# Delta-rule attention followed by mixture of depths on one core: another order of the work, six block inverses on VectorE, rank counts on TensorE

## The chip, the cores and the metric

The kernel runs on one core of a Trainium2 chip. Five engines work on their own queues, each in the order in which its instructions were written: TensorE (PE), VectorE (DVE), ScalarE (ACT), GpSimd (POOL) and SyncE (SP, which here only issues DMAs). An instruction that waits holds up everything behind it on its engine. The metric is the device time of one execution in microseconds (us), and the lower the better.

## The reference, cut to what matters

```
# attention: B=4, H=8, S=768, D=48; k_n = k / (|k| + 1e-6); state starts at zero
for t in range(S):
    y[:, :, t] = q[:, :, t] @ state                       # with the state before step t
    v_old = state^T k_n[t]
    state = state + beta[t] * outer(k_n[t], v[t] - v_old)
# bridge: x[b, s] = the 8 heads of y side by side (384 numbers)
# mixture of depths: per batch row b
scores = x[b] @ w_gate                                    # 768 scores
top = the 128 tokens with the largest scores
out[b] = x[b]; out[b, top] += sigmoid(scores[top]) * (relu(x[b, top] @ w1) @ w2)   # 384 -> 1024 -> 384
```

The 768 steps depend on each other, so they are worked in chunks of 64 tokens: inside a chunk the steps are joined through the inverse of a unit triangular 64x64 matrix per head, and only the 48x48 states pass from chunk to chunk.

## The kernel before, in words

**Units.** The batch rows are worked in two groups (rows 0 and 1, then rows 2 and 3), each of 12 chunks: 24 units, 0 to 23. A unit covers one chunk of 64 tokens for 2 rows x 8 heads. `prep` loads k and q, transposes them on TensorE (L388, copied by ScalarE at L392) and forms the products k k^T and k q^T (L405, copied at L414); GpSimd masks the second (L422). `recur` is the chain from state to state: r (L634), the subtraction on DVE (`sub`, L638), w (L646), its copies (L652), s (L660) and the new state (L666). Beside it stand q (L673) and p (L683), whose sum is the output x (L689), written to DRAM (L696). `vh` (L626, DVE) scales V before that.

**Inverses.** The triangular matrices of four units are inverted together, six times: inverse 0 for units 0 to 3, and so on to inverse 5 for units 20 to 23. `eliminate` moves the lower right halves into its buffer `a` by a DVE transpose (`turn_in`, L484; the data are shifted into place by DMA first, L433), takes norms with a root on ScalarE (L490), scales (L509), does 30 elimination steps of two instructions each (L523 and L527), applies the mask table (`final`, L533), and turns the result out (`turn_out`, L537; `turn_back`, L542). `join` (z at L587, j at L598) makes 64x64 inverses out of the 32x32 halves, and then the four units can run. Inverses 0, 2, 4 and 5 run their steps on DVE with one operand in PSUM (`pa`, filled by ScalarE at L514); inverses 1 and 3 (`POOL_E`) run on GpSimd, in SBUF.

**Depths.** `depths(b)` does the mixture for one row: scores (L701 on GpSimd and L708 on ScalarE), all scores spread over the partitions (L771, L780, L787), the rank of each token by comparing and counting on DVE (`ranks`, L813 and L818, in two stages: the first four blocks of 128 tokens, and the other two), the selection (`choose`, L826), its indices (L833), a gather (L848), the two layers on TensorE (L864, L878) with copies on ScalarE, and a scatter that adds the result to the output (L887).

**Order.** The class `Plan` sets the order in which each engine's instructions are written: every piece of work is an `Op` with an engine, a duration that is written down, what it waits for, the buffers it takes and gives back, and a priority given by a formula at each call (`u` in the functions above). `Plan.order` steps through planned time and picks the most urgent piece that can start; `Plan.fill` puts spare matmuls (L963) into planned gaps of TensorE. The three PSUM banks `inv` are shared by nearly all that TensorE makes outside the chain.

Of the kernel before, what the change touches and what calls it, by code (L numbers as in the profile page):

```python
# [25 lines left out]
class Plan:  # L26
# [56 lines left out]
    def fill(self, start, end, done):  # L83

        slots = self.rings["inv"]
        k = min(range(len(slots)), key=lambda x: slots[x])
        t = max(start, slots[k]) + 0.1
        while t + 0.6 < end:
            op = Op()
            op.eng, op.start, op.end, op.take, op.give, op.seq = "PE", t, t + 0.25, k, [], -1  # L90
            self.fills.append(op)
            t += 0.45

    def order(self):
        free, ready, last, done, self.fills = {}, {}, {}, [], []
# [5 lines left out]
        while len(done) < len(self.ops):  # L101
# [10 lines left out]
            if op.eng == "PE":  # L112
                self.fill(free["PE"], at, done)
# [38 lines left out]
def kernel(  # L152
# [57 lines left out]
    POOL_E = (1, 3)  # L210
# [22 lines left out]
    ring("a", 2, [HC, HC])  # L233
# [5 lines left out]
    ring("sel", 1, [NT, P])  # L239
    ring("xe", 2, [DM])  # L240
# [8 lines left out]
    psta = psum.tile([P, GI, 2 * D], FP32, name="psta")  # L249
# [12 lines left out]
    pe, act, dve, pool, sp = [maker(e) for e in ("PE", "ACT", "DVE", "POOL", "SP")]  # L262

# [19 lines left out]
    warm = sbuf("warm", [256], BF16)  # L283
# [18 lines left out]
    tmp = [sbuf(f"tmp{m}", [HC * HC // 4]) for m in range(2)]  # L302
# [10 lines left out]
    def constants():  # L313
# [6 lines left out]
        nc.vector.memset(psta, 0.0)  # L320
# [4 lines left out]
        for t in rings["tt"]:  # L325
# [8 lines left out]
        for t in count:  # L334
            nc.vector.memset(t, 0.0)
# [39 lines left out]
    def gk(e):  # L375
        return "g2" if e == 2 else "g"
# [58 lines left out]

    def prep(i):
        e = i // BC
        u = 40 * (e - 1) + 2 * (i % BC) - 40 * (e in POOL_E)
# [3 lines left out]
        n["lk"] = kq_on[0](1.3, load(i, "k", kq_on[1]), prio=u - 30, take=[("k", i)], lat=2.2)  # L442
# [550 lines left out]
```

## Time and profile before

| | |
|---|---|
| median of 3 runs | 409.05 us (408.43 to 413.15) |
| profiled execution | 409.91 us, its span 408.1 us |
| TensorE, matmuls | 323.1 us busy (79%) |
| TensorE, weight loads | 270.1 us (66%) |
| VectorE | 218.1 us (53%) |
| ScalarE | 179.0 us (44%) |
| GpSimd | 154.3 us (38%) |
| DMA | 32.19 MB, mean 79 GB/s |

The span runs from the first to the last instruction of the execution. Busy times of different engines overlap. No engine is busy all the time, so the shares alone tell no bound: one has to follow which engine works alone at what time. TensorE's clock is granted at one of two levels, 2.4 GHz (1.00 in the rows) and 1.2 GHz (0.50); a number between is the mean over a stretch.

### The profile page before, as it was taken

What the parts mean: (1) busy time and instruction counts of PE and PEld (TensorE: products, weight loads), DVE (VectorE), ACT (ScalarE), POOL (GpSimd) and SP (SyncE); (2) the same over time, 40 slices, a digit from 0 to 9 for tenths busy, and PEclk for the clock granted to TensorE, in tenths of its full rate; (3) what the DMA queues carried; (4) which work ended last, traced back from release to release, by engine and by line L of the source; (5) the groups of instructions that cost most, each with busy time, mean ns of one, the idle gap of its engine ahead of it and who ended that gap; (6) DMA issues with size and microseconds to landing.
All of it is one profiled execution on the core that took longest, in us unless ns stands there. A gap on an engine that the chain in (4) does not pass through costs nothing. (4 is left out here: it accounts for less than half of the span.)

```text
span 408.1 us, 14040 instructions
## 1 busy us (share of the span) xinstructions
PE 323.1 (79%) x5969; PEld 270.1 (66%) x5969; DVE 218.1 (53%) x573; ACT 179.0 (44%) x477; POOL 154.3 (38%) x239
## 2 busy tenths in 40 slices
PE   4885887689738899988489987799905998793993
PEld 3764675578627898976359876698605995663871
DVE  3004889948789211223877778958894006773000
ACT  2342564357724446566356573454202545110120
POOL 5012557888830156986832134021310014111011
PEclk9999776759975558996965899659965568696898
DMA  9847747333567233656742444133311013002011
GB/s 126 140 81 134 133 87 140 62 68 78 111 122 128 44 69 70 189 119 161 181 93 50 88 99 78 29 58 83 59 39 29 2 27 74 1 2 39 19 22 20
DMA packets 141855, 32.19 MB, mean 79 GB/s; under 512 B 139664, under 2 KB 141216, under 8 KB 141792
## 3 DMA queue, kind: packets, MB, share of 16 engines
q1 hardware_dynamic: 134432, 28.64, 35.3%
q0 software_dynamic: 960, 1.59, 2.2%
q10 hardware_dynamic: 6400, 1.05, 1.9%
q8 instruction: 47, 0.77, 0.7%
q14 instruction: 16, 0.13, 0.1%
HBM read 22.61 MB, written 5.51 MB: 69 GB/s over the span
## 5 line engine op out<-in xcount | busy, mean ns | idle before, releaser
L701 POOL TENSOR_TENSOR xw<-x,wg 128x384 f32<-128x384 f32 x23 | 23.5, 1024 | 101.4 <-ACT x L689 99.9
L422 POOL TENSOR_SCALAR_AFFINE_SELECT p<-p 64x512 f32<-64x512 f32 x44 | 31.9, 726 | 43.6 <-ACT p L414 36.9
L523 DVE TENSOR_TENSOR tmp<-a,pa 128x30 f32<-128x30 f32 (+14 forms) x120 | 39.0, 325 | 8.1 <-ACT pa L514 4.7
L527 DVE TENSOR_TENSOR pa<-pa,tmp 128x30 f32<-128x30 f32 (+14 forms) x120 | 40.6, 338 | 4.1
L392 ACT COPY kq<-inv 128x512 f32<-128x512 f32 x44 | 25.2, 589 | 37.6 <-PE inv L388 36.0
L638 DVE TENSOR_TENSOR r<-v,prec 128x384 f32<-128x384 f32 x22 | 12.1, 552 | 54.3 <-PE prec L634 45.6
L405 PE MATMUL inv<-kq 48*64 48x128 f32 (+1 forms) x832 | 37.6, 311 | 2.7 <-ACT p L414 1.6
L626 DVE TENSOR_TENSOR v<-v,nnT 128x384 f32<-128x384 f32 x24 | 19.3, 809 | 32.1 <-DMA v<-in_v_dram 32.0
L405 PEld LDWEIGHTS inv<-kq 48*64 48x64 f32 x832 | 29.1, 172 | 11.0 <-issue 4.5
L646 PE MATMUL prec<-r,tt 64*64 64x48 f32 x704 | 32.0, 251 | 4.2 <-ACT tt L603 2.0
L388 PE MATMUL inv<-ident,q 128*128 128x128 f32 x96 | 21.5, 371 | 16.4 <-DMA q<-in_q_dram 11.6
L527 POOL TENSOR_TENSOR a<-a,tmp 128x30 f32<-128x30 f32 (+14 forms) x60 | 32.7, 545 | 4.7
L813 DVE TENSOR_SCALAR_CACHE_REDUCE junk<-rep,tok 128x256 bf16<-128x256 f32 (+4 forms) x60 | 31.7, 528 | 3.5 <-ACT rep L787 1.5
L587 PE MATMUL inv<-tt,g 32*32 32x32 f32 x640 | 18.4, 227 | 18.6 <-DVE tok L801 13.0
L646 PEld LDWEIGHTS prec<-r,tt 64*64 64x64 f32 x704 | 29.0, 166 | 6.0 <-DVE r L638 2.4
L652 ACT COPY wbd<-prec 64x384 f32<-64x384 f32 x48 | 22.7, 472 | 20.6 <-PE prec L646 19.2
L523 POOL TENSOR_TENSOR tmp<-a 128x30 f32<-128x30 f32 (+14 forms) x60 | 29.4, 490 | 4.1
L388 PE MATMUL inv<-ident,k 128*128 128x128 f32 x96 | 21.3, 367 | 12.1 <-DMA k<-in_k_dram 9.5
L587 PEld LDWEIGHTS inv<-tt,g 32*32 32x32 f32 x640 | 16.6, 141 | 21.0 <-DVE tok L801 13.1
L388 PEld LDWEIGHTS inv<-ident,q 128*128 128x128 f32 x96 | 15.6, 192 | 20.4 <-DMA q<-in_q_dram 6.0
L864 PE MATMUL inv<-xeT,w_sb 128*128 128x128 f32 x192 | 25.9, 299 | 2.0 <-ACT p L414 1.0
L864 PEld LDWEIGHTS inv<-xeT,w_sb 128*128 128x128 f32 x192 | 24.8, 212 | 3.2 <-ACT xeT L858 1.8
(110 smaller groups left out, 619.6 us busy)
## 6 DMA issues: line engine op xcount, KB each, us to landing
v<-in_v_dram SPq DMA_DIRECT2D x48, 96.0 KB
out_dram<-x SPq DMA_DIRECT2D x96, 48.0 KB
k<-in_k_dram SPq DMA_DIRECT2D x44, 96.0 KB
q<-in_q_dram SPq DMA_DIRECT2D x44, 96.0 KB
ks<-in_k_dram SPq DMA_DIRECT2D x44, 96.0 KB
tt<-tt SPq DMA_DIRECT2D x12, 128.0 KB
w_sb<-in_moe_w_dram SPq DMA_DIRECT2D x4, 384.0 KB
w_sb<-in_moe_w_dram SPq DMA_DIRECT2D x3, 512.0 KB
```

The source lines that it names most:

```text
L388: nc.tensor.transpose(ps[:, r * P:(r + 1) * P], x[:, 2 * r:2 * r + 2].rearrange("p b d -> p (b d)"), ident)
L392: nc.scalar.copy(got(kk(i), i)[:, :, o], got("inv", i, nm).rearrange("p (r t) -> p r t", t=P))
L405: nc.tensor.matmul(bank(i, w, rt)[half[par], r, o], lhsT=kq[ds[rt], r, 0, half[par]], rhs=kq[ds[rt], r, o, half[par]], start=True, stop=True)
L422: nc.gpsimd.affine_select(out=t[half[par]], in_=t[half[par]], pattern=[[0, GP], [1, C]], base=0, channel_multiplier=-1, compare_op=ALU.is_ ...
L523: eng.tensor_tensor(out=t, op=ALU.mult, in0=a[:, j + 1:, j:j + 1].to_broadcast([P, w, j]), in1=x[:, j:j + 1, :j].to_broadcast([P, w, j]))
L527: eng.tensor_tensor(out=x[:, j + 1:, :j], in0=x[:, j + 1:, :j], in1=t, op=ALU.subtract)
L587: nc.tensor.matmul(ps[lo[par], b], lhsT=g[hi[par], n0 + b, :HC], rhs=tt[hi[par], n0 + b, HC:], start=True, stop=True)
L646: nc.tensor.matmul(pw[half[par], a % 2, a // 2], lhsT=tt[half[par], ch * GP + a], rhs=x[half[par], a], start=True, stop=True)
L652: nc.scalar.copy(wb[half[par], :, par].rearrange("p (r b) d -> p b r d", b=2), pw[half[par]])
L701: nc.gpsimd.tensor_tensor(out=got("xw", i), in0=got("x", i), op=ALU.mult, in1=wg[:, None, :].to_broadcast([P, GB, DM // 2]))
L813: nc.vector.tensor_scalar(out=junk[:, :(y - x) * P], in0=rows[:, x * P:y * P], scalar1=mine, scalar2=None, op0=op, op1=ALU.add, accum_out= ...
L864: nc.tensor.matmul(got("inv", b, "h", f // 2)[:, f % 2 * CAP:(f % 2 + 1) * CAP], lhsT=w1_sb[:, t, f * P:(f + 1) * P], rhs=got("xeT", b)[:, ...
```

## The change

All edits stand together in one version.

- The priority of each piece is no longer the formula's. `Plan.rank` plans once with the old priorities, then gives every piece the length of the longest way from it to the end (through those that wait for it and through those that take a buffer after it), and the work is planned again by these. DMAs are planned as pieces of their own engine, each after its issue (`moved`).
- All six inverses run on DVE with one operand in PSUM. There is one buffer `a` in place of two. `POOL_E` is gone.
- V is scaled on GpSimd.
- Ranks: three of the four rows compare on GpSimd (row 2 on DVE). The comparisons are written as 0 or 1 in bf16 into a new buffer `cmp`, and TensorE counts them by matmuls with a column of ones (20 in the first stage of a row, 22 in the second).
- Units 0 to 3 are shifted by DVE copies, not by DMA, and their q loads are put behind the k loads.
- One ScalarE copy takes the place of two in `join` (L592).
- Spare matmuls write an unused part of the state's PSUM bank (128 columns, in pairs) and not the banks `inv`, and are placed where little planned work stands in the microseconds before.

```diff
-    def fill(self, start, end, done):
-
-        slots = self.rings["inv"]
...
+    def fill(self):
+        ops = sorted((o for o in self.ops if o.eng == "PE"), key=lambda o: o.start)
...
+                near = sum(min(y, t) - max(x, t - 3.4) for x, y in work[-40:] if y > t - 3.4)
+                if near < 2.4:
...
+    def rank(self):
+        slots, refs = {n: len(s) for n, s in self.rings.items()}, dict(self.refs)
+        self.order()
...
+            tail[op.seq] = op.dur + max(
+                [tail[u.seq] + (op.lat if u.eng != op.eng else 0.0) for u in op.users] +
+                [tail[u.seq] + 0.15 for u in then.get(op.seq, []) if u.seq in tail] + [0.0])
+        for op in self.ops:
+            hot = op.prio < -500 and op.eng != "PE"
+            op.prio = -tail[op.seq] - (1000 if hot else 0)
...
     def emit(self, filler):
+        self.rank()
...
-    ring("a", 2, [HC, HC])
+    ring("a", 1, [HC, HC])
...
+    ring("cmp", 1, [22 * P], BF16)
...
+    def moved(eng, dur, size, emit, deps=(), prio=0.0, take=(), give=(), lat=1.9):
+        issue = eng(dur, emit, deps, prio, take, lat=0.3)
+        return plan.add("DMA", size, lambda: None, [issue], 0.0, give=list(give), lat=lat)
...
+    def shift0(i):
+        def emit():
...
+            for par in range(2):
+                nc.vector.tensor_copy(t[lo[par], ms, HC:], t[lo[par], ms, :HC])
...
         if first:
-            n["sh"] = act(1.3, shift(i, 1, nc.scalar), done, u, lat=2.5)
+            n["sh"] = dve(0.85, shift0(i), done, u)
...
     def eliminate(e):
-        on_pool = e in POOL_E
-        u = 40 * (e - 1) + 8 - 60 * on_pool
-        eng, run = (nc.gpsimd, pool) if on_pool else (nc.vector, dve)
+        u = 40 * (e - 1) + 8
...
-                eng.tensor_tensor(
+                nc.vector.tensor_tensor(
...
-            last = run(dur, emit, [last], u + 1000 * on_pool)
+            last = dve(dur, emit, [last], u)
...
         def ez():
-            for par in range(2):
-                nc.scalar.copy(got(gk(e), e)[lo[par], n0:n0 + GP, :HC], view(key[0])[lo[par]])
+            nc.scalar.copy(got(gk(e), e)[:P - HC, n0:n0 + GP, :HC], view(key[0])[:P - HC])
...
         def vh():
             t = got("v", i)
-            nc.vector.tensor_tensor(
+            nc.gpsimd.tensor_tensor(
...
-        r["vh"] = dve(0.57, vh, [n["lv"], N["e", e]["sc"]], u - 8)
+        r["vh"] = pool(1.05, vh, [n["lv"], N["e", e]["sc"]], u - 8)
...
+        on, eng = (dve, nc.vector) if b == 2 else (pool, nc.gpsimd)
...
-        def ranks(j, a, e):
+        def compare(j, a, e):
...
-                        nc.vector.tensor_scalar(
-                            out=junk[:, :(y - x) * P], in0=rows[:, x * P:y * P],
-                            scalar1=mine, scalar2=None, op0=op, op1=ALU.add,
-                            accum_out=cnt[:, j, (3 if a > 0 and j < a else o):][:, :1])
+                        eng.tensor_scalar(
+                            out=cmp[:, at + x * P:at + y * P], in0=rows[:, x * P:y * P],
+                            scalar1=mine, scalar2=None, op0=op)
...
+        def number(j0, j1):
+            def emit():
...
+                            nc.tensor.matmul(ps[:, t:t + 1], lhsT=cmp[:, x:x + P],
+                                             rhs=warm[:, :1], start=first, stop=True,
+                                             skip_group_check=True)
...
-    def filler(m):
-        nc.tensor.matmul(rings["inv"][m][:, :256], lhsT=warm[:, :P], rhs=warm, start=True, stop=True)
+    def filler():
+        for _ in range(2):
+            nc.tensor.matmul(pfull[:, GI * 2 * D:], lhsT=warm, rhs=warm, start=False,
+                             stop=True, skip_group_check=True)
```

Since a planner writes the order, the diff doesn't show it. Two places of it follow, as the built programs have it (a row: line, operation, written tile <- read tiles, size, and how many of them in a row; the numbers in names are buffers).

**GpSimd, at inverse 3.** Before, the queue holds the mask table of inverse 1 (made behind its steps), a product for scores (L701), and then the steps of inverse 3 on `a` (L523, L527):

```order
L502 AFFINE_SELECT mb_102<-bh_141 128x1024
L701 TENSOR_TENSOR xw_107<-x_105,wg 128x384
L523 TENSOR_TENSOR tmp_143<-a_101 128x30
L527 TENSOR_TENSOR a_101<-a_101,tmp_143 128x30
L523 TENSOR_TENSOR tmp_143<-a_101 128x58
L527 TENSOR_TENSOR a_101<-a_101,tmp_143 128x29x2
```

Now, while inverse 3 runs on DVE, the queue holds the scaling of V (L674), the scores' products (L749) and the comparisons of row 0 (L870, L879, L881):

```order
L674 TENSOR_TENSOR v_72<-v_72,nnT_137 128x384
L674 TENSOR_TENSOR v_73<-v_73,nnT_137 128x384
L870 TENSOR_SCALAR cmp_110<-rep_107,tok_127 128x128
L870 TENSOR_SCALAR cmp_110<-rep_107,tok_127 128x384
L879 TENSOR_SCALAR cmp_110<-rep_107,tok_127 128x128
L881 AFFINE_SELECT cmp_110<-cmp_110 128x128
```

The inverse's steps left this queue; work that units wait for (L674) stands in it among comparisons.

**DVE, from inverse 3 to inverse 4.** Before, the result of inverse 3 is turned out between the selection of row 0 and the start of inverse 4, whose first part (L484, `turn_in`) stands ahead of it:

```order
L824 TENSOR_REDUCE rank<-count_155 128x6
L826 TENSOR_TENSOR sel_110<-iota_r,rank 128x768
L484 STREAM_TRANSPOSE a_100<-g_99 128x1024
L486 TENSOR_SCALAR nrm<-a_100 128x32
L838 CAST idx_158<-inv_116 128x1
L844 TENSOR_SCALAR gate_162<-gate_162 128x1
L845 RECIPROCAL gate_162<-gate_162 128x1
L533 TENSOR_TENSOR a_101<-a_101,mb_102 128x1024
L537 STREAM_TRANSPOSE tt_103<-a_101 128x32x32
```

Now inverse 3's last steps (L575, L579) are followed at once by its end and by inverse 4, and the subtraction of a unit (L686) stands among the steps:

```order
L686 TENSOR_TENSOR r_144<-v_73,prec 128x2x4x48
L575 TENSOR_TENSOR tmp<-a_100,pa 128x58
L579 TENSOR_TENSOR pa<-pa,tmp 128x2x29
L575 TENSOR_TENSOR tmp<-a_100,pa 128x30
L579 TENSOR_TENSOR pa<-pa,tmp 128x30
L585 TENSOR_TENSOR a_100<-pa,mb_101 128x1024
L589 STREAM_TRANSPOSE tt_103<-a_100 128x32x32
L594 STREAM_TRANSPOSE g_98<-a_100 128x32x32
L858 COPY tok_127<-inv_118 128x4
L536 STREAM_TRANSPOSE a_100<-g_99 128x1024
```

All six inverses now stand on DVE one behind the other in this way, with three or four subtractions within each from inverse 1 on; the last four units (20 to 23) follow the end of inverse 5.

**TensorE, behind unit 23.** Before, the last matmuls of unit 23 (L646, L673, L683) are followed by spreads (L780), the indices of row 1 (L833) and then the layers of rows 1, 2 and 3; those of row 0 stand farther ahead:

```order
L646 MATMUL prec<-r_145,tt_103 64x48 x16
L673 MATMUL inv_116<-s_148,kq_84 64x48 x16
L780 MATMUL inv_118<-sel_110,ones 128x512
L683 MATMUL inv_116<-wbd_147,p_95 64x96 x8
L963 LDWEIGHTS warm
L963 MATMUL inv_117<-warm 128x256
L833 MATMUL inv_117<-tok_128,sel_110 128x2 x6
```

Now the queue has, from the last matmuls of unit 23 (L694, L721, L731) on, the layers of row 0 (L941 transposes, L951 first, L965 second layer) and then those of rows 1, 2 and 3:

```order
L721 MATMUL inv_116<-s_147,kq_83 64x48 x8
L694 MATMUL prec<-r_144,tt_103 64x48 x16
L721 MATMUL inv_116<-s_147,kq_83 64x48 x8
L941 MATMUL inv_117<-ident,xe_111 128x128 x3
L731 MATMUL inv_116<-wbd_146,p_95 64x96 x8
L951 MATMUL inv_118<-xeT_113,w_sb 128x128 x6
L951 MATMUL inv_117<-xeT_113,w_sb 128x128 x6
L965 MATMUL inv_116<-w_sb,hT_114 128x384
```

All four rows' layers stand behind unit 23; before, one row's stood ahead of it.

## Rows read from the trace of the kernel before

**Rows 1.** The page, part 1: busy us (share) x instructions.

```profile
PE 323.1 (79%) x5969; PEld 270.1 (66%) x5969; DVE 218.1 (53%) x573; ACT 179.0 (44%) x477; POOL 154.3 (38%) x239
```

**Rows 2.** Timeline of DVE: start us, us, instruction, [idle before <- releaser].

```profile
30.42 1.94 DVE L484 STREAM_TRANSPOSE a<-g 128x1024 f32<-128x1024 f32 x1 [25.93 <-ACT kq L392]
...
74.03 1.95 DVE L537 STREAM_TRANSPOSE tt<-a 128x1024 f32<-128x1024 f32 x1
...
121.64 1.94 DVE L537 STREAM_TRANSPOSE tt<-a 128x1024 f32<-128x1024 f32 x1
...
211.46 1.95 DVE L537 STREAM_TRANSPOSE tt<-a 128x1024 f32<-128x1024 f32 x1
...
254.90 1.91 DVE L537 STREAM_TRANSPOSE tt<-a 128x1024 f32<-128x1024 f32 x1
...
304.99 1.90 DVE L537 STREAM_TRANSPOSE tt<-a 128x1024 f32<-128x1024 f32 x1
```

**Rows 3.** Timeline of GpSimd: first and last pair's instructions of inverse 3.

```profile
141.60 0.25 POOL L523 TENSOR_TENSOR tmp<-a 128x30 f32<-128x30 f32 x1
...
204.03 0.25 POOL L527 TENSOR_TENSOR a<-a,tmp 128x30 f32<-128x30 f32 x1
```

**Rows 4.** Stretches: busy us (x) of each engine, clock, DMA share, GB/s.

```profile
42.00:341.00 299.00, 244.66 (x5378) 209.79 (x5378) 184.18 (x447) 152.85 (x417) 131.70 (x203) 0.75 0.42 86
341.00:408.10 67.10, 49.08 (x267) 38.16 (x266) 24.37 (x103) 11.11 (x26) 11.31 (x12) 0.82 0.12 21
...
126.00:156.00 30.00, 27.76 (x612) 25.41 (x614) 10.98 (x16) 13.74 (x37) 9.23 (x20) 0.50 0.37 69
156.00:180.00 24.00, 23.06 (x761) 21.07 (x760) 4.29 (x9) 16.73 (x50) 19.84 (x30) 1.00 0.59 145
```

**Rows 5.** Timeline of TensorE: the transposes of unit 3's k.

```profile
13.40 1.09 PE L388 MATMUL inv<-ident,k 128*128 128x128 f32 x4 [0.75 <-DMA k<-in_k_dram]
```

**Rows 6.** Timeline of DVE: end of inverse 0, and the head of inverse 1.

```profile
38.10 0.18 DVE L494 TENSOR_SCALAR nrm<-nrm 128x32 f32<-128x32 f32 x1 [5.06 <-ACT nrm L490]
...
54.95 1.96 DVE L484 STREAM_TRANSPOSE a<-g 128x1024 f32<-128x1024 f32 x1 [0.22 <-issue]
...
60.87 0.09 DVE L511 MEMSET a<- 128x32 f32 x1
...
61.70 0.40 DVE L523 TENSOR_TENSOR tmp<-a,pa 128x240 f32<-128x240 f32 x1
...
72.78 1.23 DVE L533 TENSOR_TENSOR a<-pa,mb 128x1024 f32<-128x1024 f32 x1
...
78.07 1.96 DVE L484 STREAM_TRANSPOSE a<-w_sb 128x1024 f32<-128x1024 f32 x1
```

**Rows 7.** Groups by line: out<-in xcount | busy us, mean ns | idle before, releasers.

```profile
L514 ACT COPY pa<-a 128x1024 f32<-128x1024 f32 x4 | 4.0, 1009 | 0.8 <-DVE a L511 0.8
L638 DVE TENSOR_TENSOR r<-v,prec 128x384 f32<-128x384 f32 x22 | 12.1, 552 | 54.3 <-PE prec L634 45.6 <-ACT junk L708 8.6
L626 DVE TENSOR_TENSOR v<-v,nnT 128x384 f32<-128x384 f32 x24 | 19.3, 809 | 32.1 <-DMA v<-in_v_dram 32.0
L701 POOL TENSOR_TENSOR xw<-x,wg 128x384 f32<-128x384 f32 x23 | 23.5, 1024 | 101.4 <-ACT x L689 99.9 <-PE inv L795 1.1
L502 POOL TENSOR_SCALAR_AFFINE_SELECT mb<-bh 128x1024 f32<-128x1024 f32 x6 | 8.8, 1462 | 23.0 <-DVE bh L498 14.3 <-DVE a L533 4.7 <-DVE nnT L499 4.0
L963 PEld LDWEIGHTS <-warm 128*128 128x128 bf16 x69 | 7.3, 115 | 5.4 <-issue 2.9 <-DVE r L315 1.3
L833 PEld LDWEIGHTS inv<-tok,sel 128*128 128x128 f32 x48 | 7.0, 227 | 1.6 <-DVE sel L826 1.3
```

**Rows 8.** Timeline of TensorE behind unit 23: rows 2 and 3 through both layers.

```profile
373.54 0.90 PE L854 MATMUL inv<-ident,xe 128*128 128x128 f32 x3 [7.16 <-DMA xe<-out_dram,idx]
...
389.37 0.49 PE L854 MATMUL inv<-ident,xe 128*128 128x128 f32 x3
...
396.08 5.33 PE L878 MATMUL inv<-w_sb,hT 128*128 128x384 f32 x16
```

More of the change, by code (lines that the diff above doesn't have):

```diff
@@ L81, in pick @@
         return min(fits or urgent, key=lambda c: (c[1].prio, c[1].seq))
-    def fill(self, start, end, done):
-        slots = self.rings["inv"]
[L86 to L92, printed above, removed]
+    def fill(self):
+        ops = sorted((o for o in self.ops if o.eng == "PE"), key=lambda o: o.start)
+        used = [(a.start - 0.1, b.end + 0.1) for a, b in self.spans]
+        fills, work, t, last = [], [], 0.0, max(o.end for o in ops)
+        for op in ops + [None]:
+            end = op.start if op else last
+            while t + 0.15 < end:
+                if any(a < t < b for a, b in used):
+                    t += 0.1
+                    continue
+                near = sum(min(y, t) - max(x, t - 3.4) for x, y in work[-40:] if y > t - 3.4)
+                if near < 2.4:
+                    fill = Op()
+                    fill.eng, fill.start, fill.end, fill.give, fill.seq = "PE", t, t, [], -1
+                    fills.append(fill)
+                    work.append((t, t + 0.3))
+                t += 0.3
+            if op:
+                work.append((op.start, op.end))
+                t = max(t, op.end)
+        return fills
     def order(self):
-        free, ready, last, done, self.fills = {}, {}, {}, [], []
+        free, ready, last, done = {}, {}, {}, []
         for op in self.ops:
@@ L139, in emit @@
             if op.seq < 0:
-                filler(op.take)
+                filler()
                 continue
@@ L301 @@
     bh = [sbuf(f"bh{m}", [HC]) for m in range(2)]
-    tmp = [sbuf(f"tmp{m}", [HC * HC // 4]) for m in range(2)]
+    tmp = sbuf("tmp", [HC * HC // 4])
     rhs = [sbuf(f"r{m}", [GP, D]) for m in range(2)]
@@ L441, in prep @@
         kq_on = (act, nc.scalar) if first and i % 2 else (sp, nc.sync)
-        n["lk"] = kq_on[0](1.3, load(i, "k", kq_on[1]), prio=u - 30, take=[("k", i)], lat=2.2)
-        n["lq"] = kq_on[0](1.3, load(i, "q", kq_on[1]), prio=u - 20, take=[("q", i)], lat=2.2)
+        late = 34 if first else 0
+        n["lk"] = moved(kq_on[0], 1.3, 1.15, load(i, "k", kq_on[1]), prio=u - 30,
+                        take=[("k", i)])
+        n["lq"] = moved(kq_on[0], 1.3, 1.15, load(i, "q", kq_on[1]), prio=u - 29 + late,
+                        take=[("q", i)])
         for o, nm in enumerate("kq"):
@@ L763, in depths @@
         stages = ((0, 4), (4, NT))
+        on, eng = (dve, nc.vector) if b == 2 else (pool, nc.gpsimd)
+        place = {}
+        for j0, j1 in stages:
+            x = 0
+            for j in range(j1):
+                a = 0 if j >= j0 else j0
+                place[j, a] = (x, x + (j1 - a) * P)
+                x += (j1 - a + (j >= j0)) * P
         m = {}
```

161 lines of the change are left out of this document (99 added, 62 removed).

## The prediction, written before the result was known

> **What bounds the kernel now.** I read the page first. No engine carries the span: TensorE is busy for 323.1 us, DVE for 218.1, GpSimd for 154.3 [rows 1]. The chain of waits is of no help here, since it reaches back over the last scatters only. So I went to the timelines and asked what the units wait for. The six `turn_out` instructions tell it: inverse 0 is out at 76.0 us, inverses 2 and 1 at 123.6 and 126.6, inverse 3 at 213.4, inverse 4 at 256.8, inverse 5 at 306.9 [rows 2]. Four units wait for each. The longest step, to inverse 3, is GpSimd's: its steps, with masks and products between them, run from 141.6 to 204.3 us, 62.7 us [rows 3]; from 156 to 180 us DVE is busy for 4.29 of 24 us [rows 4]. So the bound up to 341 us, where the last matmul of unit 23 ends, is the string of inverses with its pauses; behind it come 67.1 us of tail in which TensorE is busy for 49.08 [rows 4].
>
> **The change, part by part.** The new order puts six inverses on DVE one behind the other. So I add: the start, inverse 0, five periods from one inverse to the next, the last four units, the tail.
>
> *Start.* Inverse 0 begins at 30.4 us today [rows 2], because q loads and later units' k stand ahead of the shifts. The k of unit 3 is transposed by 14.5 us already [rows 5], and behind it come a copy, the products, their split and now a DVE copy, some 3 us. I take 17.5. The bounds are 16 and, if nothing comes of the new load order, 30.4.
>
> *One inverse.* The last 15 of 30 steps run from 61.70 to 72.78 us, 11.1 us; the first 15 have the same sizes in mirrored order, so 22.2 [rows 6]. `final` and both turns up to the next `turn_in` take 78.07 - 72.78 = 5.3; the head, from 54.95 to 60.96, takes 6.0, of which 1.1 is a pair of steps of the inverse before, so 4.9 [rows 6]; the fill of `pa` by ScalarE adds 1.0 and a handover of 0.1 [rows 7]. The sum is 33.5 us, or 31.4 up to the end of `turn_out`. Inverse 0 has no units beside it, but ScalarE's root may come late (5.06 us today [rows 6]); I add 1. It is out at 17.5 + 31.4 + 1 = 50 us.
>
> *A period.* To the 33.5 come 19 subtractions of 0.55 us over five periods, 2.1 each [rows 7], so 35.6. V's scaling leaves (809 ns each, with 32.0 us of waits for its loads [rows 7]). What stays are waits inside the queue: for ScalarE's root and fill, and for r from TensorE. Today inverse 2 takes from 78.07 to 123.58, 45.5 us [rows 2, 6]: over 31.4 that is 14.1, of which four subtractions are 2.2 and five scalings 4.0, so 7.9 are waits. Part of these were for V's loads. Between 0 and 7.9 I take 5, because the waits for V go but the queues of ScalarE and TensorE are fuller than today. A period is 40.6 us, and inverse 5 is out at 50 + 5 x 40.6 = 253 us.
>
> *The last four units.* Today 341 - 306.9 = 34 us [rows 2, 4], of which most runs at 1.2 GHz. Records per busy us are 612 / 27.76 = 22.0 in a stretch at 0.50 and 761 / 23.06 = 33.0 at 1.00 [rows 4], so the full clock makes such work shorter by a third; 34 x 0.67 = 23, and some waits stay. Bounds 25 and 34, I take 31: unit 23 ends at 284 us.
>
> *Tail.* All four rows' layers now stand behind unit 23 on TensorE. Row 3's took 401.41 - 389.37 = 12.0 us from its transposes on, row 2's, partly at the lower clock, 389.37 - 373.54 = 15.8 [rows 8]. Four at 12.0 are 48. The counts are new: 64 of 168 one-column matmuls lie here, and nothing shows their price; the nearest row is the 115 ns of a bf16 weight load, the far one the 227 ns of an fp32 one [rows 7]. 64 x 0.115 = 7.4, of which I put 4 on the path, because part fills pauses for ScalarE. From the last matmul to the end today: 408.1 - 401.4 = 6.7. With 2 taken off for layers that now overlap, the tail is 57 us (bounds 50 and 4 x 15.8 + 7.4 + 6.7 = 77). Comparing and choosing for rows 2 and 3 is covered by the 24 us of rows 0 and 1; without that cover it would show by some 10 us.
>
> *What I cost at nothing.* GpSimd loses two inverses of 62 us and gains 24 scalings at 1.02 us (the same shape as L701 [rows 7]), 25 us. Its comparisons have no row: per row some 5,400 elements a partition in 20 instructions, besides six masks. At L701's pace (1024 ns for 384) that is 14 us and up, at the mask table's (1462 for 1024 [rows 7]) about 8; so three rows cost 24 to 43, and GpSimd is busy for 140 to 160 us of 340. Its cover is that slack. ScalarE loses 24 copies, DVE most of its ranking. Spare matmuls are 88 of 128 columns in place of 69 of 256.
>
> *Sum.* 284 + 57 = 341 us of span. The profiled execution lies 1.8 above its span and 0.9 above the median, so I predict **342 us**.
>
> *A cross-check, which is also the weak point.* TensorE is busy for 244.7 us from 42 to 341 at a mean clock of 0.75 [rows 4], half the time at either level. Without row 0's layers (12) and with 104 counts (12) the same work is 245, so at today's clock it fills 42 to 287 us without a pause. Both bounds fall together, and a small loss on one shows. By the ratio above the work is 122 + 122 x 0.67 = 204 us at the full clock and 306 at the half, per four units 34 and 51. The clock decides whether TensorE holds up the inverses.
>
> From 126 to 156 us TensorE was busy for 27.76 of 30 us and the clock stood at 1.2 GHz all the time [rows 4]. The Trainium skill ("TensorE: Matmul & The Clock Gate", Part 1) says that the throttled clock is the default and that activity releases it; by that, a TensorE with hardly a pause would run at 2.4 GHz, and the time would be that of the second rival. The row speaks against relying on it.
>
> **The rivals.**
> 1. *TensorE holds up the string* (24%). The joins behind each inverse run at 1.2 GHz as today, ScalarE stands waiting for TensorE, and root, fill and subtractions on DVE come late. For it: 45.6 us of today's waits before subtractions are for r [rows 7]. Periods like today's inverse 2, 45.5: 50 + 227 + 33 + 59 + 1 = 370 us; in part, 357 to 375.
> 2. *The clock stays up* (18%). With work at hand TensorE needs 34 us of each period; waits shrink to 1.5, periods to 37: 50 + 185 + 27 + 55 + 1 = 318 us. Against it: the stretch above.
> 3. *GpSimd comes late* (7%). A unit's V stands behind a stage of comparisons (4 to 9 us) at some four places, and w waits: 342 + 20 = 362 us. For V's scaling this row is the nearest: 1024 ns on GpSimd for what took DVE 809 in the mean [rows 7]. The Trainium skill ("GPSIMD Engine Reference", Engine selection) speaks against such a move, two-input work being about twice as slow there, and calls one-input work nearly line rate; by that, comparisons cost the lower price.
> 4. *Slower* (2%): all at 1.2 GHz. Then four units need 51 us of TensorE and, with joins that wait, a period 53: 50 + 265 + 40 + 75 + 1 = 431 us. It decides from periods of 50 us on. Against it: more work at hand than today, when half the time ran at the full clock.
> 5. *The order does not what it says* (3%): the start stays at 30 us and the waits at 7.9: 62 + 5 x 43.5 + 31 + 57 + 1 = 369 us.
>
> **How the numbers follow.** The forecast has 46%, as 332 to 356 us. The range takes in most of rivals 1 to 3 and 5: **318 to 372 us**; outside stay the faster half of rival 2, the tops of 1 and 3, and rival 4. A difference of 2%, 8 us, is about what can be told from no change; 401 us and less is faster. Faster 0.96, same 0.02, slower 0.02.
>
> **What would show it.** In the profile of the changed kernel: first `turn_in` on DVE near 17.5 us; six `turn_out` on DVE, the first out at 50, the last near 253, 40 us apart; DVE waits inside an inverse near 5 us; unit 23's last matmul near 284; TensorE without a pause from there to 335, the last layers 12 us a row; GpSimd near 140 us busy. The prediction is wrong in its first term if inverse 0 starts at 25 or later, in its main term if the periods are not 36 to 46, and in the last if rows 2 and 3 wait for ranks behind unit 23. A mean clock below 0.7 or above 0.9 would move it to rivals 1 or 2.

## The result, and the profile after

The changed kernel takes **367.2 us** (median of four runs, 363.8 to 378.9) against 409.2 us beside it: a ratio of 0.893 (95% interval 0.882 to 0.903). The forecast was 342 us with a range of 318 to 372. The direction and the range held; the point was 25 us too low. The profiled execution took 365.55 us with a span of 363.7 us. Medians are over all runs of a kernel, while ratios leave out the runs in its slower state, in which the granted clock is lower and the time longer (here 378.9 us at 0.758, the other three at 0.783 to 0.809).

The page of the changed kernel, busy time by engine and four of its groups (they answer to [rows 1, 7]):

```profile
PE 311.0 (86%) x6156; PEld 267.2 (73%) x6156; DVE 212.5 (58%) x538; ACT 168.8 (46%) x453; POOL 173.4 (48%) x221
...
L575 DVE TENSOR_TENSOR tmp<-a,pa 128x30 f32<-128x30 f32 (+9 forms) x180 | 58.9, 327 | 21.2 <-ACT pa L566 15.7
...
L674 POOL TENSOR_TENSOR v<-v,nnT 128x384 f32<-128x384 f32 x24 | 20.8, 867 | 82.3 <-DMA v<-in_v_dram 50.7
L870 POOL TENSOR_SCALAR cmp<-rep,tok 128x256 bf16<-128x256 f32 (+5 forms) x42 | 46.5, 1119 | 7.5 <-PE inv L894 7.4
...
L686 DVE TENSOR_TENSOR r<-v,prec 128x384 f32<-128x384 f32 x22 | 12.1, 551 | 23.9 <-PE prec L682 12.7
```

DVE does about as much as before although all six inverses run on it: V's scaling and three rows' comparisons stand on the POOL lines now. The waits have moved as well. Before, 45.6 us of DVE's idle time ended with r from TensorE [rows 7]; now that is 12.7, and 15.7 end with the fill of `pa` by ScalarE.

The timeline of DVE in the changed kernel, the first `turn_in` (L536), the six `turn_out` (L589) and one step of an inverse (they answer to [rows 2]):

```profile
19.80 1.95 DVE L536 STREAM_TRANSPOSE a<-g 128x1024 f32<-128x1024 f32 x1
...
50.59 1.94 DVE L589 STREAM_TRANSPOSE tt<-a 128x1024 f32<-128x1024 f32 x1
...
90.33 1.94 DVE L589 STREAM_TRANSPOSE tt<-a 128x1024 f32<-128x1024 f32 x1
...
107.32 0.20 DVE L575 TENSOR_TENSOR tmp<-a,pa 128x30 f32<-128x30 f32 x1 [7.60 <-ACT pa L566]
...
135.91 1.97 DVE L589 STREAM_TRANSPOSE tt<-a 128x1024 f32<-128x1024 f32 x1
...
175.50 1.96 DVE L589 STREAM_TRANSPOSE tt<-a 128x1024 f32<-128x1024 f32 x1
...
215.68 2.00 DVE L589 STREAM_TRANSPOSE tt<-a 128x1024 f32<-128x1024 f32 x1
...
262.18 1.94 DVE L589 STREAM_TRANSPOSE tt<-a 128x1024 f32<-128x1024 f32 x1
```

The ends are 52.5, 92.3, 137.9, 177.5, 217.7 and 264.1 us, the periods 39.7, 45.6, 39.6, 40.2 and 46.4. The last matmul of unit 23 ends at 298.8 us (before: 341). So 23.5 us of the gain were there when inverse 0 was out (52.5 for 76.0 [rows 2]), and 19.3 came in the five periods (211.6 for 230.9).

Stretches of the changed kernel (columns as in [rows 4]): the string, the last four units, the tail, and a piece of 36 us across the first border:

```profile
20.00:264.00 244.00, 207.79 (x4840) 181.14 (x4838) 186.62 (x459) 132.21 (x359) 120.22 (x149) 0.78 0.54 110
264.00:300.00 36.00, 35.59 (x780) 31.43 (x781) 11.88 (x32) 18.18 (x49) 21.62 (x27) 0.73 0.19 43
300.00:363.70 63.70, 53.49 (x357) 42.47 (x355) 6.92 (x26) 11.77 (x31) 25.62 (x29) 0.90 0.13 22
247.00:283.00 36.00, 35.19 (x644) 32.04 (x640) 15.45 (x39) 13.93 (x40) 21.60 (x24) 0.50 0.25 54
```

### The profile page after: what moved, and what is told of

The parts are those of the page before. It is cut to its first block, busy times and chain, and to the rows that moved or that the text cites. A ratio compares the mean times of both kernels' runs of the same rounds, so it can differ in the third digit from the quotient of the medians.

```text
span 363.7 us, 14373 instructions
## 1 busy us (share of the span) xinstructions
PE 311.0 (86%) x6156; PEld 267.2 (73%) x6156; DVE 212.5 (58%) x538; ACT 168.8 (46%) x453; POOL 173.4 (48%) x221
## 3 DMA queue, kind: packets, MB, share of 16 engines
q1 hardware_dynamic: 134432, 28.64, 39.8%
## 5 line engine op out<-in xcount | busy, mean ns | idle before, releaser
L575 DVE TENSOR_TENSOR tmp<-a,pa 128x30 f32<-128x30 f32 (+9 forms) x180 | 58.9, 327 | 21.2 <-ACT pa L566 15.7
L579 DVE TENSOR_TENSOR pa<-pa,tmp 128x30 f32<-128x30 f32 (+9 forms) x180 | 60.8, 338 | 6.2
L674 POOL TENSOR_TENSOR v<-v,nnT 128x384 f32<-128x384 f32 x24 | 20.8, 867 | 82.3 <-DMA v<-in_v_dram 50.7
L870 POOL TENSOR_SCALAR cmp<-rep,tok 128x256 bf16<-128x256 f32 (+5 forms) x42 | 46.5, 1119 | 7.5 <-PE inv L894 7.4
L749 POOL TENSOR_TENSOR xw<-x,wg 128x384 f32<-128x384 f32 x23 | 23.2, 1011 | 33.3 <-ACT x L737 12.6
L694 PE MATMUL prec<-r,tt 64*64 64x48 f32 x704 | 31.2, 245 | 4.7 <-ACT tt L651 3.0
L694 PEld LDWEIGHTS prec<-r,tt 64*64 64x64 f32 x704 | 28.0, 159 | 8.1 <-ACT tt L651 3.4
L700 ACT COPY wbd<-prec 64x384 f32<-64x384 f32 x48 | 22.7, 473 | 22.5 <-PE prec L694 17.8
L721 PE MATMUL inv<-s,kq 48*64 48x48 f32 x640 | 30.6, 258 | 1.6 <-ACT w_sb L640 1.6
L951 PEld LDWEIGHTS inv<-xeT,w_sb 128*128 128x128 f32 x192 | 26.6, 208 | 5.1 <-ACT xeT L945 1.1
L721 PEld LDWEIGHTS inv<-s,kq 48*64 48x64 f32 x640 | 28.2, 174 | 3.0 <-ACT w_sb L640 1.7
L951 PE MATMUL inv<-xeT,w_sb 128*128 128x128 f32 x192 | 27.9, 295 | 0.0
L708 PE MATMUL psta<-wbd,ks 128*48 128x96 f32 x352 | 24.2, 294 | 3.2 <-ACT wbd L700 3.2
L686 DVE TENSOR_TENSOR r<-v,prec 128x384 f32<-128x384 f32 x22 | 12.1, 551 | 23.9 <-PE prec L682 12.7
L731 PE MATMUL inv<-wbd,p 128*64 128x96 f32 x352 | 25.1, 301 | 1.1 <-POOL p L465 1.0
L965 PE MATMUL inv<-w_sb,hT 128*128 128x384 f32 x64 | 25.4, 500 | 0.0
L708 PEld LDWEIGHTS psta<-wbd,ks 128*48 128x48 f32 x352 | 19.2, 149 | 6.4 <-ACT wbd L700 4.7
```

What stands on the lines that cost most here:

```text
L575: nc.vector.tensor_tensor(out=t, op=ALU.mult, in0=a[:, j + 1:, j:j + 1].to_broadcast([P, w, j]), in1=x[:, j:j + 1, :j].to_broadcast([P, w, ...
L579: nc.vector.tensor_tensor(out=x[:, j + 1:, :j], in0=x[:, j + 1:, :j], in1=t, op=ALU.subtract)
L694: nc.tensor.matmul(pw[half[par], a % 2, a // 2], lhsT=tt[half[par], ch * GP + a], rhs=x[half[par], a], start=True, stop=True)
L708: nc.tensor.matmul(psta[ds[a % 2], a // 2], lhsT=t[:, a, :D], rhs=wb[:, a].rearrange("p h d -> p (h d)"), start=(c == 0 and a < 2), stop=True,
L721: nc.tensor.matmul(y[half[rt], (2 * a + par) * D:(2 * a + par + 1) * D], lhsT=kq[ds[rt], a, 1, half[par]], rhs=s_old[ds[rt], a, par], star ...
L731: nc.tensor.matmul(y[half[a % 2], (a // 2) * 2 * D:(a // 2 + 1) * 2 * D], lhsT=t[:, a], rhs=wb[:, a].rearrange("p h d -> p (h d)"), start= ...
```

## The experiments

Each ratio is against the kernel before, run beside the kernel of the experiment.

**The changed kernel again**, as the reference for the shorter inverses, the lighter TensorE and the missing spare matmuls below: 

> The changed kernel again, as the reference for the other three of this call. All theories: 364 to 369 us.

Measured: 368.1 us, ratio 0.896 (0.887 to 0.906).

**The move of the inverses alone**, in the kernel before:

```
-    POOL_E = (1, 3)
+    POOL_E = ()
```

> The kernel before with one thing changed: inverses 1 and 3 on DVE in PSUM as the others; hand-written order, ranks on DVE, loads and the scaling of V as before. Theory (the move of the inverses alone isn't the gain, since over half of the 44 us came from inverse 0 being out 23.5 us earlier, which hangs on the loads and the order): 390 to 410 us. Rival (the move alone does it: GpSimd's inverse of 62.7 us was what the units waited for): 368 to 380 us.

(In the order that comes out, inverse 2's norms overwrite inverse 1's before they are used; the instructions and their sizes are the same.) Measured: 419.4 us (413.4 to 423.1), with the kernel before at 413.6 (404.5 to 417.5): no gain. The first `turn_out` ended at 63.3, the last at 315.2 us, a period of 50.4. Three groups of DVE in this kernel:

```profile
L813 DVE TENSOR_SCALAR_CACHE_REDUCE junk<-rep,tok 128x256 bf16<-128x256 f32 (+4 forms) x60 | 31.6, 527 | 3.2 <-ACT rep L787 1.5
L626 DVE TENSOR_TENSOR v<-v,nnT 128x384 f32<-128x384 f32 x24 | 17.6, 740 | 13.2 <-DMA v<-in_v_dram 13.0
L638 DVE TENSOR_TENSOR r<-v,prec 128x384 f32<-128x384 f32 x22 | 12.2, 552 | 53.5 <-PE prec L634 50.7 <-ACT nrm L490 2.8
```

Ranks and V's scaling stand between the steps of the inverses, and the waits for r are 50.7 us. That GpSimd's 62 us of inverse pay on DVE only when DVE's other work moves off is how I read this; with the old order no run moved it off.

**The hand-written priorities** in the changed kernel:

```
     def emit(self, filler):
-        self.rank()
```

> The changed kernel with the priorities written by hand in place of the longest way to the end; all else as changed. In its DVE row the subtractions of three units stand ahead of the turn_in of inverses 3 and 4, where the ranked order has them one by one inside the next inverse's steps. Theory (the order holds the string of inverses together): the string waits there for two units' chains each time, 8 to 14 us twice, and the time is 385 to 395 us against 367. Rival (the gain is the engine that the inverses run on, and the order adds little): 362 to 372 us, with periods of inverses as now, 40 to 46 us.

Measured: 436.9 us (430.6 to 441.8), ratio 1.061 (1.040 to 1.081), slower than the kernel before (404.5 to 417.5 beside it) and beyond what either theory gave. DVE's timeline between inverses 2 and 3 of this kernel, in the longest of its six executions:

```profile
156.80 0.55 DVE L685 TENSOR_TENSOR r<-v,prec 128x384 f32<-128x384 f32 x1 [11.00 <-ACT w_sb L639]
...
163.89 0.56 DVE L685 TENSOR_TENSOR r<-v,prec 128x384 f32<-128x384 f32 x1 [0.46 <-PE prec L681]
...
169.49 0.55 DVE L685 TENSOR_TENSOR r<-v,prec 128x384 f32<-128x384 f32 x1 [0.56 <-PE prec L681]
169.96 1.96 DVE L535 STREAM_TRANSPOSE a<-g 128x1024 f32<-128x1024 f32 x1
```

The next `turn_in` stands behind three units' subtractions: 169.96 us, when inverse 2 was out at 143.8. The periods there are 57.9 and 59.6 us. With the hand-written priorities the string on DVE does not hold together; whether others by hand would do was not run. The first `turn_out` ended at 52.2 us here too, so the earlier start does not hang on the new order.

**V's scaling on DVE again**, in the changed kernel:

```
         def vh():
...
-            nc.gpsimd.tensor_tensor(
+            nc.vector.tensor_tensor(
...
-        r["vh"] = pool(1.05, vh, [n["lv"], N["e", e]["sc"]], u - 8)
+        r["vh"] = dve(0.57, vh, [n["lv"], N["e", e]["sc"]], u - 8)
```

> The changed kernel with V scaled on DVE again, as before. Theory (the string on DVE is the bound, so 20 scalings of 0.6 to 0.8 us inside it lengthen it, with waits for loads on top): 5 periods x 4 x 0.8 = 16 us more, 378 to 386 us. Rival (TensorE is the bound where it has no pause, half of the time, and DVE has room there): 366 to 372 us.

Measured: 393.3 us (393.0 to 393.5), ratio 0.968 (0.958 to 0.978): 26 us lost against the 367.2 above (the changed kernel was not run beside it), more than the 16 of the first theory. `turn_out` ended at 56.2 first and at 287.6 us last, so the periods sum to 231.4 against 211.6; 15.3 us of scaling brought 17.4 us of waits for its loads:

```profile
L674 DVE TENSOR_TENSOR v<-v,nnT 128x384 f32<-128x384 f32 x24 | 15.3, 637 | 17.4 <-DMA v<-in_v_dram 17.4
```

**Row 3's comparisons on DVE**, in the changed kernel:

```
-        on, eng = (dve, nc.vector) if b == 2 else (pool, nc.gpsimd)
+        on, eng = (dve, nc.vector) if b >= 2 else (pool, nc.gpsimd)
```

> The changed kernel with row 3's comparisons on DVE, as row 2's are already. In the changed kernel they stand behind row 0's scatter on GpSimd and end at 328.6 us; TensorE idles 2.8 us at 324 to 330 and then runs at 1.2 GHz for 6. Theory (the tail is held by GpSimd there): the count is in by 316 us, TensorE has no hole, and the time falls by 4 to 7 us, to 360 to 363 if the kernel as changed runs at 367 beside it. Rival (the tail is TensorE's 54 us of work, whatever the ranks do): within 2 us.

Measured: 367.7 us (363.8 to 372.9), ratio 0.898 (0.878 to 0.917): in the time, no difference that can be told. In the trace (369.7 us) the hole is gone (TensorE was at the full clock from 308 to 356 us), and from unit 23's last matmul to the end are 60.9 us against 64.9. In that execution the clock had stayed at 1.2 GHz from 268 to 302 us, and the units ended 8 us later. For the tail the theory holds, in one execution: 4.0 of its 4 to 7 us, where the rival has none. The four times (363.8 to 372.9 us, at mean clocks of 0.802 down to 0.760) lie too far apart to decide.

**Shorter inverses** (every second subtraction left out):

```
-                nc.vector.tensor_tensor(out=x[:, j + 1:, :j], ...
+                if j % 2 == 0:
+                    nc.vector.tensor_tensor(out=x[:, j + 1:, :j], ...
```

> The changed kernel with its order, but the subtraction of every second step of each inverse left out (the odd ones, 15 of 30, some 5 us of DVE per inverse, 30 us in all); what is computed is no longer an inverse. Theory D (the string on DVE is the bound up to inverse 5, and each us in it shows): six times 5 us less, 335 to 342 us. Rival P (TensorE at 1.2 GHz sets the periods, DVE waits for it): the waits for fill, root and r take up most of it, and the time falls by at most 10 us, 356 to 364.

Measured: 369.3 us, ratio 0.898 (0.888 to 0.908). DVE has 29 us less to do and **nothing** is gained. What DVE waited for in this kernel from 47 to 271 us (us in total, times, longest):

```profile
DVE r L687 <- PE prec L683: 26.4, 11, 5.9
DVE tmp L575 <- ACT pa L566: 17.9, 5, 8.3
DVE r L687 <- ACT tt L652: 17.3, 4, 5.5
DVE nrm L546 <- ACT nrm L542: 9.5, 5, 8.5
```

All waits sum to 80 us against 43 in the changed kernel beside it. Subtractions stand at written places between the steps; a quicker step waits at the next subtraction. DVE is not the bound by itself.

**Less TensorE work** (half of the output matmuls left out, in `mm_q` and in `mm_p`):

```
-                for a in range(n * GI // 2, (n + 1) * GI // 2):
+                for a in range(n * GI // 2, n * GI // 2 + 1):
-            for a in range(GP):
+            for a in range(GP // 2):
```

> The changed kernel with its order, but half of the matmuls that make the units' outputs left out (q with the state, P with w: 320 and 176 of them, 15 and 13 us of TensorE's busy time, over all units); the outputs are not the reference's. Theory D (the string on DVE is the bound up to 264 us): the periods keep their 40 to 46 us or lose 1 or 2 each, the last four units, where TensorE has no pause, lose 6 to 8: 350 to 360 us. Rival P (TensorE holds up the string, and that is the miss of 25 us against the 342 forecast): 336 to 346 us, with periods near 37.

Measured: 361.0 us, ratio 0.878 (0.867 to 0.889): 7 us for 28 us of matmuls. TensorE was busy for 300.1 us instead of 313.9, half of what the removed work took; the mean granted clock was lower, 0.756 to 0.778 in the four executions against 0.793 to 0.805. So the run took away only half of the busy time that it was meant to. The gain sits in the fifth period (37.4 us for 46.7); the first four together are 3.6 us longer. TensorE's work is not the bound of the whole string by itself; the time is just above the first theory's range, but that theory had failed on the shorter inverses.

**No spare matmuls:**

```
-        return sorted(done + self.fill(), key=lambda o: (o.start, o.seq))
+        return sorted(done, key=lambda o: (o.start, o.seq))
```

> The changed kernel without the spare matmuls that the planner puts into TensorE's pauses; all else as changed. Theory (they hold TensorE's clock up in the pauses): a lower mean granted clock than 0.81, and 372 to 385 us. Rival (the clock falls in stretches where TensorE is busy anyway, 243 to 284 us, so they do nothing): within 4 us of the changed kernel beside it.

Measured: 366.4 us (361.8 to 376.2), ratio 0.885 (0.874 to 0.897). The rival's time holds: they do nothing that can be measured.

**Where the waits of 7.6 us come from.** Around 95 us of the changed kernel, SP's queue shows DMA issues without a gap:

```profile
88.90 3.11 SPq L411 DMA_DIRECT2D q<-in_q_dram  x4
92.11 1.34 SPq L476 DMA_DIRECT2D g<-g  x2
93.49 2.75 SPq L318 DMA_DIRECT2D bt<-in_beta_dram  x4
96.34 1.32 SPq L476 DMA_DIRECT2D g<-g  x2
97.71 1.33 SPq L385 DMA_DIRECT2D wg<-in_moe_w_gate_dram  x2
99.13 1.34 SPq L600 DMA_DIRECT2D tt<-tt  x2
100.57 1.87 SPq L411 DMA_DIRECT2D v<-in_v_dram  x2
```

ScalarE's timeline there:

```profile
102.56 0.82 ACT L651 COPY tt<-inv 32x256 f32<-32x256 f32 x2 [5.34 <-DMA tt<-tt]
...
106.27 1.01 ACT L566 COPY pa<-a 128x1024 f32<-128x1024 f32 x1
```

And the busy share of the DMA engines in 40 slices from 86 to 110 us:

```profile
DMA  6867787728768821000652659973677743333333
```

`turn_out` ended at 92.3, and its result is moved by the DMA issued at 99.13. ScalarE's copy waits for that, the fill of `pa` stands behind the copy, and DVE behind the fill. Meanwhile, from 94.4 to 97.4 us (slices 15 to 19), the DMA engines are nearly idle: four issues of 4 KB each take 2.75 us.

**The move issued by ScalarE** (in `move`, and where the planner gets it):

```
-                nc.sync.dma_start(out=t[lo[par], :, :HC], ...
+                nc.scalar.dma_start(out=t[lo[par], :, :HC], ...
-        s["mv"] = moved(sp, 1.3, ...
+        s["mv"] = moved(act, 1.3, ...
```

> The changed kernel with one thing changed: the two DMAs that move tt behind each turn_out are issued by ScalarE in place of SP. In the changed kernel SP issues them 6.7, 4.6, 5.4, 1.2 and 0 us after the turn_out of inverses 1 to 5, since loads and stores stand ahead; ScalarE waits up to 5.9 us for their landing, and the fill of pa for the next inverse stands behind that wait, so that DVE idles up to 7.5 us. Theory M (this late move is what holds both the string and the units): waits of DVE for the fill fall from 15 us to under 5, and the time falls by 8 to 14 us, to 354 to 360 against 368. Rival C (the units' own chain through TensorE at 1.2 GHz is as long as a period anyway): the wait goes elsewhere, the subtractions above all, and the time stays within 4 us.

Measured: 372.7 us, ratio 0.908 (0.899 to 0.916), against 0.896 (0.887 to 0.906) of the changed kernel above: no gain.

**The same with the shorter inverses:**

> The kernel with the move on ScalarE, and besides every second subtraction inside the inverses left out as in the short-inverse run, which removed 30 us of DVE and no time. Theory M (in that run the late move pinned the periods): with the move early the shorter steps show, some 3 us each in six inverses, and the time is 12 to 20 us under that of the kernel with the move alone, 338 to 348. Rival C (the units' chain is the bound as soon as DVE is quicker): within 5 us of the kernel with the move alone, and DVE's waits before subtractions grow by what the inverses lost.

Measured: 373.3 us (369.2 to 377.0) in the median. Its two faster runs, 369.2 and 369.9, are 3 us under those of the move alone (372.1 to 372.7), far from the 12 to 20 of theory M. DVE's waits in it, 47 to 262 us:

```profile
DVE nrm L546 <- ACT nrm L542: 20.9, 5, 11.1
DVE r L687 <- PE prec L683: 19.5, 9, 4.0
...
DVE tmp L575 <- ACT pa L566: 7.8, 4, 3.3
```

The fill's wait fell from 17.9 to 7.8 us and the root's rose from 9.5 to 20.9: ScalarE's queue now holds a score (its product comes from GpSimd, which waits up to 12.5 us for a load of V) ahead of the root. Theory M falls. The late move was one late DMA among others; in this trace the load of V was another.

**A version meant to be faster:** the move on ScalarE, row 3 on DVE, `final` and `turn_out` as one step of the planner (a row's second-stage comparisons also wait for its first-stage ones):

```
-        last = dve(1.25, final, [last, s["mb"]], u, give=[("mb", e), ("A", e)])
-        s["to"] = last = dve(1.95, turn_out, [last], u, take=[("tt", e)])
+        s["to"] = last = dve(3.2, final, [last, s["mb"]], u, take=[("tt", e)], give=...)
```

> A version meant to be faster: the move on ScalarE, row 3's comparisons on DVE, and final and turn_out placed as one step so that nothing stands between them on DVE. From the traces: 8 to 14 us for the move, 3 to 4 for the hole in TensorE at the ranks of row 3, 2 to 4 for inverse 5: 348 to 356 us. By rival C (the units' chain through TensorE is the bound): 360 to 366.

Measured: 374.1 us, ratio 0.905 (0.894 to 0.916). A failure: not faster than the change, and outside both ranges.

**Fewer issues on SP** (in `load`):

```
-            for par in range(2):
+            for par in range(0 if nm in ("q", "ks") and i >= 6 else 2):
```

> The changed kernel with every engine's order as it is, but the loads of q and of the second copy of k left out from unit 6 on, so that these units work on stale tiles (their outputs are not the reference's). What is open: less DVE work, less TensorE work and an earlier move each took away a suspected bound and the time stayed at 361 to 373. In the changed kernel SP's own queue shows DMA issues of 0.7 to 0.8 us one behind the other, 37.8 us of 39, 42.9 of 45, 38.7 of 40, 35 of 43 and 39.3 of 47 in the five stretches from inverse to inverse. Theory S (SP's issues are the hidden string: V, shifts and moves come late behind them, and with them everything else): some 68 issues fewer, about 12 a period, and the periods shrink towards DVE's 36: 335 to 350 us. Rival C (the chain of the units through TensorE at 1.2 GHz, ScalarE and DVE in their written order is as long as a period by itself): 360 to 370 us, with SP's queue standing half empty.

Measured: **351.3 us** (348.7 to 352.5), ratio 0.850 (0.842 to 0.857): 17 us under the 368.1 of the changed kernel above (not run beside it), the largest gain of all the runs, with every other engine's instructions in the same order. DVE's first and last `turn_out` in it:

```profile
49.62 1.97 DVE L589 STREAM_TRANSPOSE tt<-a 128x1024 f32<-128x1024 f32 x1
...
245.82 1.92 DVE L589 STREAM_TRANSPOSE tt<-a 128x1024 f32<-128x1024 f32 x1
```

Its DVE waits, 52 to 248 us:

```profile
DVE r L686 <- PE prec L682: 10.3, 6, 3.2
DVE tmp L575 <- ACT pa L566: 6.5, 4, 3.3
DVE r L686 <- ACT tt L651: 3.7, 2, 3.0
DVE nrm L546 <- ACT nrm L542: 2.6, 5, 1.4
```

The periods sum to 196.2 us against 213.4 in the changed kernel run again, 39.2 each, and DVE's waits to 27 against 43: the 16 us of waits are nearly all of the gain. The durations of SP's issues, added up between the ends of `turn_out`, are 38.3 us of 39.8 in the changed kernel, then 42.3 of 45.6, 39.0 of 39.6, 35.2 of 40.2 and 33.3 of 46.4 (256 issues, 0.73 us in the mean); here 140.3 of 196.2 (192 issues, 0.73 us). Pauses of the queue that one row of the timeline spans are taken out of these sums; the 39.3 of 47 us in the expectation has 6 us of them in it.

So SP's queue is full or nearly so in the first four periods, and not in the fifth, the longest: there it stands idle for 11.7 us. Against the changed kernel run again, the periods shrink from 38.8, 45.4, 39.1, 43.3 and 46.7 us to 35.5, 41.2, 39.1, 39.9 and 40.5: the third, with a full queue, by nothing, and the fifth, without one, by the most. The fifth period of the changed kernel, and the same of this one (from `turn_out` to `turn_out`, columns as in [rows 4]):

```profile
217.70:264.10 46.40, 41.75 (x944) 37.87 (x942) 32.46 (x84) 17.80 (x49) 36.38 (x43) 0.65 0.35 72
```

```profile
205.30:245.80 40.50, 35.81 (x970) 32.32 (x970) 32.80 (x83) 19.69 (x56) 33.72 (x41) 0.83 0.30 62
```

TensorE is busy for 41.75 of 46.4 us at a mean clock of 0.65, and for 35.81 of 40.5 at 0.83. The time is just above theory S's 335 to 350 us and well below rival C's 360. Theory S is borne out in part, by 11 us in the first four periods; for the 6 us of the fifth, TensorE at the lower clock is the nearer cause, and it is not shown. Left open besides: the 64 loads took their bytes along, and the units no longer wait for them, so issues, transfers and those waits aren't separated; a version with as many bytes in fewer issues wasn't run. The mean clock was 0.83 against 0.80 too, and TensorE took 301.2 us instead of 313.9 for the same 6156 instructions; whether that is cause or consequence stays open.

## Why the prediction was right, and where it was off

The terms against the profiled execution:

| Term | forecast | measured |
|---|---|---|
| inverse 0 begins | 17.5 | 19.8 |
| inverse 0 is out | 50 | 52.5 |
| five periods | 203 | 211.6 |
| last four units | 31 | 34.7 |
| tail | 57 | 64.9 |
| span | 341 | 363.7 |

All terms came out longer, by 22.7 us together, and 367.2 us lies outside the 332 to 356 to which the forecast gave its 46%. The range held because it took in the rivals, whose causes came only in part; to that extent it held by luck. What was right is the mechanism of the larger part: one string of six inverses on DVE, begun near 20 us, with periods near 40.

**Start: right in kind, 2.3 short.** The four shifts on DVE come 1.6 to 2.1 us apart, each behind a unit's split, and the last ends at 19.76. One inverse is as worked out (32.7 from `turn_in` to the end of `turn_out`, forecast 31.4 and 1 for the root).

**Periods: the work was right, the waits were mis-sized.** DVE is busy for 31.9 us of a period, and 2.3 are gaps between instructions: 34.2 against the 35.6 of the forecast. The waits are 8.1 against 5, just over the bound of 7.9. They are mostly the waits that the forecast named (fill 14.7, r 11.7, root 5.8 of 40.6 us in all). By period they are 5.6, 11.9, 4.8, 6.5 and 11.7: the miss sits in the second and the fifth. In the second, 7.6 us are the fill behind the late move, and the reason that the forecast gave, "the queues of ScalarE and TensorE are fuller", is not theirs. The step that failed there is *What I cost at nothing*. It went through GpSimd, ScalarE, DVE and TensorE and left out SP, whose queue was nearly full in the kernel before as well (52 issues, 35.5 us, from 52 to 91 us). Shortening the string to periods of 40 us met a queue with 35 to 42 us of issues in each of the first four. Relieved of 64 issues, the period was 39.2 us, below the forecast 40.6. In the fifth period SP's queue was not full, and the cause of its waits stays open; both runs in which TensorE was busy for less there, at a higher clock, shortened it (37.4 us with half of the output matmuls: 30.1 busy at 0.80; 40.5 with fewer loads).

**V's scaling.** It was put to 25 us on GpSimd and took 20.8. That it hangs on late loads (82.3 us of idle time ahead of it) costs GpSimd little; on DVE it would cost 26 us of time.

**Last four units: mis-sized by 3.7.** The forecast scaled the 34 us of the kernel before by the clock. The mean clock was 0.73 in this stretch (264.1 to 298.8 us) against 0.61 before (306.9 to 341), and the units' own matmuls were busy for 26.5 us instead of 30.9. What the forecast left out is work of the mixture that now stands among them on TensorE, 11.2 us against 1.4; its two largest groups, changed kernel, 244 to 300 us (both lie behind 264):

```profile
L920 PE MATMUL inv<-tok,sel 128*128 128x2 f32 x24 | 5.4, 354 | 0.0
...
L837 PE MATMUL inv<-sel,ones 128*128 128x512 f32 x4 | 2.8, 800 | 0.0
```

TensorE had next to no pause left (34.39 of 34.7 us). The clock stood at 1.2 GHz from 247 to 283 us with TensorE busy for 35.19 of 36 us, as it had from 126 to 156 us in the kernel before [rows 4]. The Trainium skill ("TensorE: Matmul & The Clock Gate", Part 1) has activity release the throttle; this stretch speaks against it again, so the second rival fell.

**Tail: mis-sized by 7.9, by the cover that the forecast named.** A row's two layers take 11.9 us (345.26 to 357.17), as forecast, and from the last matmul to the end are 6.5 us (6.7). The counts were cheaper than thought: 20 take 0.64 us at the full clock, 32 ns each for an estimate of 115. But row 3's ranks were not covered. GpSimd's timeline, changed kernel:

```profile
314.81 1.96 POOL L974 DMA_INDIRECT out_dram<-oe,idx  x1 [6.86 <-DVE count L908]
316.86 6.07 POOL L870 TENSOR_SCALAR cmp<-rep,tok 128x256 bf16<-128x256 f32 x6
...
328.30 0.29 POOL L881 TENSOR_SCALAR_AFFINE_SELECT cmp<-cmp 128x128 bf16<-128x128 bf16 x1
```

Row 3's comparisons stand behind row 0's scatter, which waits for its result, and end at 328.6. TensorE idles for 2.8 us and then runs some of its work at 1.2 GHz: the indices (`mm_idx`) take 2.56 for 1.40 us, 18 matmuls of the first layer 3.88 for 2.25. With their neighbours that is 7 of the 7.9 us. By its own test, a wait for ranks behind unit 23, the last term was wrong; the start (under 25) and four of five periods (36 to 46) passed theirs.

**GpSimd: dearer than its bounds.** The forecast was 24 to 43 us for three rows' comparisons, 20 instructions a row. They took 57.4: 46.5 for 14 instructions a row and 10.9 for the six that settle ties. Their masks took 6.9 more, and GpSimd was busy for 173 us (140 to 160). The same comparison by size on both engines, changed kernel:

```profile
L870 POOL TENSOR_SCALAR cmp<-rep,tok 128x256 bf16<-128x256 f32 x18 | 16.4, 924 | 6.8 <-PE inv L894 6.7
...
L870 POOL TENSOR_SCALAR cmp<-rep,tok 128x768 bf16<-128x768 f32 x3 | 6.6, 2210 | 0.0
...
L870 DVE TENSOR_SCALAR cmp<-rep,tok 128x256 bf16<-128x256 f32 x6 | 1.9, 370 | 1.6 <-ACT rep L844 1.6
...
L870 DVE TENSOR_SCALAR cmp<-rep,tok 128x768 bf16<-128x768 f32 x1 | 0.6, 608 | 0.0
```

512 more elements cost 1.29 us on GpSimd and 0.24 on DVE. The Trainium skill ("GPSIMD Engine Reference", Engine selection) calls one-input work there roughly line-rate; these rows differ. Up to 264 us the slack took this, but for one wait of 2.3 us that the profile puts before a subtraction at 249.7 us; in the tail it showed.

**The rivals.** The time lies in the 357 to 375 of the first one (TensorE holds up the string). As the cause of the whole miss it is not borne out: 28 us of matmuls less gave 7, though TensorE's busy time fell by half of that only. In the fifth period it is not excluded. Of the third a late GpSimd came, for 7 us, but in the tail, by comparisons that stand behind a scatter and not by V. The second and the fourth did not come. Of the fifth one half came, the waits (8.1 for its 7.9), and the late start didn't; the new order does what it says, since without it the time is 437.

## What to carry to other kernels

Count the queue that issues DMAs as an engine: number of issues by the time of one, against the period that the change aims at; it stands in no busy column. Count it stretch by stretch: a sum over the whole string hides a period in which the queue stands idle. Where several in-order queues wait for one another, taking work off one of them may give nothing: the wait moves to the next written place. Leaving work out on each queue in turn, with the order of the others unchanged, narrows down which one holds the rest, as long as the clock is read beside it. Moves between engines can be worth something only as a set: the inverses alone on DVE gained nothing, and taking back V's scaling alone cost 26 us. Before scaling a stretch by the clock, list what else the new order puts into it.

## What the runs showed of the hardware

An issue on SP's queue takes 0.65 to 0.69 us whether it moves 96 KB (V, 1.31 for two, at 50.4 us) or 4 KB (2.75 for four). Of the 337 issues of the changed kernel 30 take 1.0 us or more; what makes these longer isn't shown, and the mean between the `turn_out` was 0.73 us with 256 issues and with 192. With less TensorE work the granted clock was lower (0.764 for 0.801 in the profiled executions), and the busy time fell by half of what was removed. The clock stayed at its lower level from 247 to 283 us, while TensorE was busy for 35.19 of these 36 us.
